# Converting the feed-forward weights later and more thinly inside a top-k attention and gated feed-forward kernel

## The chip, the cores and the metric

The kernel runs on one core of a Trainium2 chip. The metric is the time of one execution on the device, in microseconds (us). The engines of the core are TensorE (PE, with its weight loads as PEld), VectorE (DVE), ScalarE (ACT), GpSimd (POOL) and SyncE (SP, which here issues all DMAs).

## The reference

Attention over 8 batches of 8 heads, 576 positions, head size 64. Each row keeps its 32 largest scores; the result is the input of a feed-forward block with a convolution over three positions as its gate. The inputs q, k, v are float32, the weights float64.

```python
scores = scale * np.matmul(q, k.transpose(0, 1, 3, 2))
kth = np.partition(scores, -top_k, axis=-1)[..., -top_k:-top_k + 1]
scores = np.where(scores >= kth, scores, -1000000000.0)
attn = softmax(scores)                        # written out in the reference
x = np.matmul(attn, v)                        # (8, 576, 512) after the heads are joined
h = np.maximum(x @ w_in, 0.0)                 # w_in 512 x 1024
conv_out = sum(conv_w[k] * shifted(h, k - 1) for k in range(3))
out = (h * 1.0 / (1.0 + np.exp(-conv_out))) @ w_out      # w_out 1024 x 512
```

## The kernel before

The work is cut into 288 attention tiles of 128 rows by 576 scores: 8 batches, 4 pairs of heads, 9 tiles a pair. A software pipeline runs over them. Iteration `it` (from -3 on) issues one stage of each of several tiles, in an order written out by hand in `iteration`; each engine runs its own instructions in just that order. For tile n the stages are: the scores on PE and their copy to memory by ACT (L218, L225) two iterations ahead; seven MAX8 over chunks on DVE at it = n (L232); five further DVE steps that narrow the candidates at n + 1 (L252, L254); the sign of each score against a threshold by ACT (`sides`, L265) and its product on POOL (`flip`, L270) at n + 2; the exponential by ACT (`expo`, L277) at n + 3; a last MAX8, the choice of the threshold and the masked weights on DVE at n + 4 (`below` L280, `select` L284, `weigh` L290); the transposes on PE (L303) and their copy at n + 5 (L308); then the product with v (L334). So the start of L290 for tile i marks iteration i + 4, and L290 is executed once in each iteration from 4 to 291.

After the nine tiles of a pair the sums are inverted on DVE (L349, L350) and sent through DRAM by SP (L358 to L364). POOL then normalises in three operations (L369 to L371) that wait in a list, `pool_tasks`. A budget decides how many of that list an iteration runs: 2.0 an iteration, less `CONV_COST` 1.5 for each weight block on POOL. When the fourth pair of a batch is normalised, the feed-forward work of the batch starts: `Expand` (L401, one of eight blocks of 128 features every two iterations, for each of two parts of the rows), the gate (L470 on DVE), `Contract` (L551). The gated activations lie in memory under the tags g0 and g1, one for each part.

The float64 weights arrive as pairs of 32-bit words. 33 blocks (conv_w, then 16 of w_in, then 16 of w_out, 128 x 256 values each) are loaded by SP (L141) and converted, one block an iteration from iteration -3. A block passes through `split` on DVE (L149, a shift of the upper word), `act` on ACT (L152, L153), `pool` on POOL one iteration later (L157 the sign, L158 an integer add, L159 the product), `lead` on ACT in that same iteration (L162, the rounded high part), and `trail` on POOL an iteration later (L165, the low part). The raw words use the buffers of the tags x_hi and x_lo, which later hold the normalised rows; the temporaries lie in `scratch`, three slots of four. `load_blocks` keeps up to 12 blocks loaded ahead. `Expand` waits until the blocks of w_in are done, and `split_next`, ahead of `Contract`, until all are.

Of the kernel before, what the change touches and what calls it, by code (L numbers as in the profile page):

```python
# [13 lines left out]
BF16 = mybir.dt.bfloat16  # L14
U16 = mybir.dt.uint16
U32 = mybir.dt.uint32
I32 = mybir.dt.int32
AF = mybir.ActivationFunctionType
ALU = mybir.AluOpType
ENG = mybir.EngineType  # L20

P = 128
# [10 lines left out]
XNB = 7  # L33
# [12 lines left out]
FEED = 1.42  # L46
CONV_COST = 1.5
W_FIRST = 4
W_LATE = 12
NORM_LAG = 2  # L50
CONV_LAG = 1
OB = 1
WB = 256
# [12 lines left out]
def attend_and_feed(ctx: ExitStack, tc: tile.TileContext, q, k, v, weights, out, shared, finish=None):  # L66
    nc = tc.nc
# [5 lines left out]
    DM, DF = wi.shape[2] * P, wi.shape[3]  # L73
    NCT = DM // P
    NFT = DF // P
# [7 lines left out]
    ROWS = [(0, NI * TAIL), (NI * TAIL, S)]  # L83
# [6 lines left out]
    xp = ctx.enter_context(tc.tile_pool(name="xp", bufs=XNB))  # L90
    moe = ctx.enter_context(tc.tile_pool(name="moe", bufs=1))
# [10 lines left out]
    for i in range(0 if exact else SB):  # L102
        side = const.tile([P, S + 3], BF16, name=f"side{i}")
# [15 lines left out]
    def bank(name):  # L119
        return ps.tile([P, BANK], F32, name=name, tag=name, bufs=1)  # L120
# [1 line left out]
    def corner(i):  # L122
        return s_ps[:, i * (P + S):i * (P + S) + P]

    scratch = []

    class Convert:
        count = 0
# [4 lines left out]
        def load(self):  # L133
            i = Convert.count
            Convert.count += 1
            if not scratch:
                scratch.append(moe.tile([P, 4 * SPB, WB], F32, name="scratch", tag="split"))
            self.at = i % SPB * 4
            tag = ("x_hi", "x_lo")[i % 2]
            self.raw = xp.tile([P, self.src.shape[-1], 2], U32, name="raw64", tag=tag)[0:self.n]  # L140
            nc.sync.dma_start(out=self.raw.rearrange("a c t -> a (c t)"), in_=self.src.bitcast(U32))  # L141

        def tmp(self, i):
            return scratch[0][0:self.n, self.at + i, 0:self.raw.shape[1]]

        def split(self):
            self.bits, self.rest, self.side = (self.tmp(i) for i in range(3))
            top = self.raw[:, :, 1]
            yield lambda: nc.vector.tensor_scalar(self.bits.bitcast(U32), top, 3, None, ALU.logical_shift_left)  # L149

        def act(self):
            nc.scalar.activation(out=self.rest, in_=self.raw[:, :, 0], func=AF.Copy, scale=2.0 ** -51, bias=2.0)  # L152
            nc.scalar.activation(out=self.side.bitcast(I32), in_=f32(self.raw[:, :, 1]), func=AF.Copy, scale=0.5 / LEAST)  # L153

        def pool(self):
            x, side = self.bits, self.side
            nc.gpsimd.tensor_scalar(side, side.bitcast(I32), 1.0, -1.0, ALU.min, ALU.max)  # L157
            nc.gpsimd.tensor_tensor(x.bitcast(U32), x.bitcast(U32), self.rest.bitcast(U32), ALU.add)  # L158
            nc.gpsimd.tensor_tensor(self.dst if self.low is None else x, x, side, ALU.mult)  # L159

        def lead(self):
            nc.scalar.copy(out=self.dst, in_=self.bits)  # L162
# [4 lines left out]
    def weight_blocks():  # L167
        w_in, conv_w, w_out = weights
        yield Convert(conv_w, P, cw.rearrange("p t f -> p (t f)"), None)
        for c in range(NCT):  # L170
            for n in range(0, DF, WB):
                yield Convert(w_in[c * P:(c + 1) * P, n:n + WB], P, wi[:, 0, c, n:n + WB], wi[:, 1, c, n:n + WB])
        for f in range(NFT):
            for n in range(0, DM, WB):
                yield Convert(w_out[f * P:(f + 1) * P, n:n + WB], P, wo[:, 0, f, n:n + WB], wo[:, 1, f, n:n + WB])
# [4 lines left out]
    def ratios():  # L180
        size(cr[:, 0], cw[:, 1])
        nc.vector.tensor_scalar(cr[:, 0], cr[:, 0], SMALL, None, ALU.is_lt)
        nc.vector.tensor_tensor(cr[:, 0], cr[:, 0], cw[:, 1], ALU.add)
        nc.vector.reciprocal(cr[:, 0], cr[:, 0])
        nc.vector.tensor_tensor(cr[:, 1], cr[:, 0], cw[:, 2], ALU.mult)
        nc.vector.tensor_tensor(cr[:, 0], cr[:, 0], cw[:, 0], ALU.mult)
# [306 lines left out]
    class Contract:  # L493
# [11 lines left out]
        def split(self):  # L505
# [3 lines left out]
            if late and len(parts) == 1:  # L509
                for pool, name, n, size in ((att, "e2", EBUFS, 2 * S), (att, "pT", 2, 2 * MAIN)):  # L510
                    for _ in range(n):
                        t = pool.tile([P, size], F32R, name=name, bufs=n)
                        extra.append(t[:, 0:2 * NFT * TAIL].rearrange("p (i c) -> p i c", i=2))
                parts.extend(extra)
# [95 lines left out]
        return expands.popleft()  # L610

    def next_contract():
        if not contracts or not contracts[0].ready:
            return None
        if contracts[0].first:
            if contracted.waiting >= (2 if state.it > NT + 4 else CB):
                return None
            contracted.waiting += 1
        return contracts.popleft()
# [13 lines left out]
    expands, contracts = deque(), deque()  # L633
    state = Box()
    state.flying = state.avs = state.it = 0
    state.due, state.tanh_at = 0.0, -9
    state.split = state.splits = state.late_splits = 0
    state.credit, state.pool = 0.0, 0.0
    lanes = expanded, contracted = Box(), Box()
    for lane, take in zip(lanes, (next_expand, next_contract)):  # L640
        lane.take, lane.cur, lane.waiting, lane.finished = take, None, 0, deque()
# [2 lines left out]
    blocks = deque()  # L644
    if weights is not None:
        blocks.extend(weight_blocks())
    state.blocks = 0 if weights is not None else NCT * DF
    fetched, cut, dved, whole, led = (deque() for _ in range(5))

    def start(pc):  # L650
# [22 lines left out]
                    lane.finished.append(lane.unit)  # L673
        return budget

    def load_blocks(n=2 * XNB - 3):
        while blocks and len(fetched) < n:
            c = blocks.popleft()
            c.load()
            fetched.append(c)  # L680

    def convert_pool():
        while led:
            led.popleft().trail()
            state.blocks += 1
        while dved:
            c = dved.popleft()
            c.pool()
            if c.low is None:
                state.blocks += 1  # L690
                ratios()
            else:
                whole.append(c)

    def convert_dve():
        ops = []
        if fetched:
            c = fetched.popleft()
            ops.extend(c.split())
            cut.append(c)  # L700
        return ops

    def convert_act():
        while cut:
            c = cut.popleft()
            c.act()
            dved.append(c)
        while whole:
            c = whole.popleft()
            c.lead()  # L710
            led.append(c)
        load_blocks(W_LATE)

    av_next, out_next, rec_next, norm_wait = [], [], [], []

    def iteration(it):
        nonlocal av_next, out_next, rec_next
        n = it + 3
# [14 lines left out]
        if n < NT:  # L733
# [3 lines left out]
            t = Box()  # L737
# [18 lines left out]
        else:  # L756
            a_ops = list(chunk_ops(tA)) if tA is not None else []
            b_ops = list(cand_ops(tB)) if tB is not None else []
        pool_used = CONV_COST * len(dved)
        convert_pool()  # L760
        c_ops = convert_dve()
        for i in range(max(7, len(a_ops), len(b_ops))):
            if i < len(a_ops):
                a_ops[i]()
# [58 lines left out]
        while pool_tasks and state.pool > 0.2 and pool_tasks[0][0] <= it:  # L823
# [3 lines left out]
            _, c, fn = pool_tasks.popleft()  # L827
# [6 lines left out]
    with tc.manual_schedule(engines=engines) if engines else nullcontext():  # L834
        load_blocks(1)
        fetch(pcs[0])
        load_blocks(W_FIRST)
        fetch(pcs[1])
        for it in range(-3, NT + 6):
            iteration(it)  # L840
    if finish is not None:
        finish(corner(2)[0:1, 0:1])
    while expands or contracts or any(x.waiting for x in lanes) or pool_tasks or tanh_next or tanh_now or gates:
        it += 1
        iteration(it)
# [3 lines left out]
def kernel(  # L849
# [32 lines left out]
    def count_lost(total):  # L882
# [19 lines left out]
        nc.vector.tensor_copy(flag, total)  # L902

    attend_and_feed(tc, q, k, (v_main, v_tail), (w_in, conv_w, w_out), out, shared, count_lost)
    lost_rows = nc.values_load(flag[0:1, 0:1])
    with tc.If(lost_rows > 0):
        attend_and_feed(tc, q, k, (v_main, v_tail), None, out, shared)
# [55 lines left out]
```

## Time and profile before

| | |
|---|---|
| median of 3 runs | 1115.03 us (1114.95 to 1115.05) |
| profiled execution, own time | 1114.6 us |
| its span on the core | 1112.7 us |
| busy share of the span | PE 90%, PEld 73%, DVE 92%, ACT 89%, POOL 80% |

The span runs from the first to the last instruction of the profiled execution; its own time is 1.9 us longer. Engines overlap, so the shares don't add up; and the share of the whole span is a mean over stages that need not have the same limit.

### The profile page before, as it was taken

How to read it: one execution, taken by the hardware profiler on the slowest of the kernel's cores; microseconds unless marked ns; L12 is line 12 of the kernel's file. 1: busy time of each engine (PE TensorE's matmuls, PEld its weight loads, DVE VectorE, ACT ScalarE, POOL GpSimd, SP SyncE). 2: the span in 40 equal slices, each digit the busy share in tenths (PEclk: the TensorE clock that was granted, in tenths of full speed). 3: DMA queues.
4: the chain of work that ended last, by engine and by line, in shares of the span. 5: the costliest groups of instructions: out<-in, count | busy, mean ns of one | idle time of the engine just before them, and what ended most of it. 6: DMA issues, size and time to landing. Idle time of an engine off the chain costs nothing.

```text
span 1112.7 us, 28088 instructions
## 1 busy us (share of the span) xinstructions
PE 1006.6 (90%) x8354; PEld 810.4 (73%) x8354; DVE 1024.9 (92%) x5768; ACT 989.6 (89%) x2342; POOL 892.1 (80%) x1078
## 2 busy tenths in 40 slices
PE   3666568889999999999999899999999999999997
PEld 2444456667788787888788777888778777887985
DVE  5998999999999999999999999999999999998551
ACT  5998888999999999999999999999999999998442
POOL 6999956889888897999887997978988897999200
PEclk9986899999999999999999999999999999999998
DMA  7221011111111111111111111111111111000001
GB/s 256 90 90 45 2 44 46 46 45 45 64 46 55 55 32 40 49 55 56 55 55 61 50 53 32 40 51 55 55 55 55 55 55 47 29 24 22 31 29 41
DMA packets 51697, 58.70 MB, mean 53 GB/s; under 512 B 9776, under 2 KB 30544, under 8 KB 51536
## 3 DMA queue, kind: packets, MB, share of 16 engines
q1 hardware_dynamic: 51536, 56.82, 16.0%
q8 instruction: 69, 1.13, 0.4%
q14 instruction: 92, 0.75, 0.2%
HBM read 47.21 MB, written 9.58 MB: 51 GB/s over the span
## 4 chain that ended last, share of the span: by engine, by line
PE 45%; DVE 38%; ACT 12%; POOL 3%; issue 2%; DMA 0%; SPq 0%; ACTq 0%; POOLq 0%
DVE cand L232 12%; PE mc L551 10%; PE me L401 9%; DVE e L290 9%; DVE z L280 7%; PE pt L303 6%; PE s_ps L334 6%; PE s_ps L218 6%; DVE cand L254 3%; ACT weights_ps L277 3%; ACT side L265 2%; PE weights_ps L551 2%; DVE rows L252 2%; DVE hot L284 2%; ACT rows L225 2%; PE s_ps L207 2%
## 5 line engine op out<-in xcount | busy, mean ns | idle before, releaser
L232 DVE MAX8 cand<-rows 128x8 f32<-128x82 f32 (+1 forms) x2016 | 453.2, 239 | 1.1 <-ACT rows L225 1.1
L270 POOL TENSOR_TENSOR z<-rows,side 128x579 f32<-128x579 f32 x288 | 347.8, 1207 | 110.4 <-ACT side L265 88.7
L277 ACT ACTIVATE weights_ps<-rows,z 128x576 f32<-128x576 f32 x288 | 219.6, 762 | 16.1 <-DVE e L290 7.5
L290 DVE SCALAR_TENSOR_TENSOR e<-rows,kth,weights_ps 128x576 f32<-128x576 f32 x288 | 230.4, 800 | 0.2
L265 ACT ACTIVATE side<-rows 128x576 bf16<-128x576 f32 x288 | 224.5, 779 | 0.3
L401 PE MATMUL me<-x_hi,wi 128*128 128x322 f32 (+1 forms) x928 | 218.3, 308 | 2.4 <-ACT g L415 1.6
L280 DVE MAX8 z<-z 128x8 f32<-128x576 f32 x288 | 214.2, 744 | 1.5 <-POOL z L270 1.5
L218 PE MATMUL s_ps<-k,q 64*128 64x384 f32 (+1 forms) x1024 | 172.5, 450 | 43.8 <-ACT xt L345 28.1
L225 ACT COPY rows<-s_ps 128x576 f32<-128x576 f32 x288 | 183.2, 636 | 21.0 <-PE s_ps L337 13.7
L303 PE MATMUL pt<-ident,e 128*128 128x128 f32 x1152 | 195.1, 293 | 2.6 <-DVE e L290 2.3
L334 PE MATMUL s_ps<-pT,vn 128*64 128x128 f32 (+1 forms) x2560 | 167.1, 274 | 26.1 <-ACT rows L225 26.0
L551 PE MATMUL mc<-wo,split 128*128 128x512 f32 x684 | 187.1, 407 | 0.2 <-ACT o L567 0.2
L218 PEld LDWEIGHTS s_ps<-k,q 64*128 64x128 f32 x1024 | 122.1, 191 | 86.2 <-ACT xt L345 37.0
L334 PEld LDWEIGHTS s_ps<-pT,vn 128*64 128x64 f32 x2560 | 130.7, 140 | 62.2 <-ACT rows L225 33.4
L303 PEld LDWEIGHTS pt<-ident,e 128*128 128x128 f32 x1152 | 125.1, 145 | 57.2 <-issue 28.9
L401 PEld LDWEIGHTS me<-x_hi,wi 128*128 128x128 f32 x928 | 156.7, 189 | 4.7 <-ACT g L415 2.8
L308 ACT COPY pT<-pt 128x512 f32<-128x512 f32 x256 | 154.6, 604 | 0.7 <-PE pt L303 0.7
L401 PE MATMUL me<-x_lo,wi 128*128 128x258 f32 (+1 forms) x464 | 138.3, 298 | 0.0
L551 PEld LDWEIGHTS mc<-wo,split 128*128 128x128 f32 x684 | 120.1, 189 | 20.4 <-ACT o L567 0.6
L434 POOL TENSOR_SCALAR t<-g,cr 128x256 f32<-128x256 f32 (+1 forms) x222 | 114.4, 515 | 0.0
L252 DVE MAX8 rows<-cand 128x8 f32<-128x21 f32 x576 | 109.6, 190 | 0.0
L448 POOL TENSOR_TENSOR t<-t,t 128x256 f32<-128x256 f32 (+1 forms) x111 | 89.2, 803 | 9.2
(116 smaller groups left out, 1673.6 us busy)
## 6 DMA issues: line engine op xcount, KB each, us to landing
k<-in_k_dram SPq DMA_DIRECT2D x32, 288.0 KB
q<-in_q_dram SPq DMA_DIRECT2D x32, 288.0 KB
vn<-in_v_main_dram SPq DMA_DIRECT2D x32, 256.0 KB
rb<-row SPq DMA_DIRECT2D x64, 128.0 KB
out_dram<-o SPq DMA_DIRECT2D x24, 256.0 KB
raw<-in_w_in_dram SPq DMA_DIRECT2D x16, 256.0 KB
raw<-in_w_out_dram SPq DMA_DIRECT2D x16, 256.0 KB
vt<-in_v_tail_dram SPq DMA_DIRECT2D x32, 64.0 KB
```

The source lines that it names most:

```text
L218: made.append(nc.tensor.matmul(s_ps[:, to + a:to + z], lhsT=qx[rows_of[h], at], rhs=kx[rows_of[h], a:z], start=True, stop=True))
L225: nc.scalar.copy(out=x, in_=s_ps[:, at:at + S])
L232: yield lambda c=c, at=at, n=n: nc.vector.max(out=t.cand[:, c:8 * CHUNKS:CHUNKS], in_=t.x[:, at:at + n])
L265: nc.scalar.activation(out=t.side[:, 2:S + 2], in_=t.x, func=AF.Sign, scale=-OVER, bias=t.row[:, 7:8], accum_out=t.cnt)
L270: nc.gpsimd.tensor_tensor(t.z[:, 8:S + 11], t.row[:, 6:S + 9], t.side, ALU.mult)
L277: nc.scalar.activation(out=e_ps, in_=t.x, func=AF.Exp, scale=scale, bias=t.shift)
L280: nc.vector.max(out=t.z[:, 0:8], in_=t.z[:, 10:S + 10])
L290: nc.vector.scalar_tensor_tensor(out=t.e, in0=t.x, scalar=kth[:, t.n:t.n + 1], in1=e_ps, op0=ALU.is_ge, op1=ALU.mult, accum_out=t.pc.sums[ ...
L303: nc.tensor.transpose(tp[:, i * P:(i + 1) * P], t.e[:, o + i * P:o + (i + 1) * P], ident)
L334: nc.tensor.matmul(a[r, 0:w], lhsT=st.pc.vn[:, h, i], rhs=st.pT[:, h if st.i < NI else 1 - h, i, 0:w], start=(i == 0), stop=False)
L401: nc.tensor.matmul(mm[:, 0:w], lhsT=wt, rhs=xx, start=(n == 0), stop=(n == len(ops) - 1))
L551: nc.tensor.matmul(mm[0:m], lhsT=x[:, i], rhs=wo[:, e, f], start=start, stop=stop)
```

## The change

The raw words go into five slots of one tile under the tag g1, which the feed-forward work writes only later, and four blocks at most are loaded ahead (12 before). conv_w is converted at iteration -3 as before. Then a counter, `state.turn`, holds the others back until iteration 2 and lets three of every four iterations convert a block. The shift becomes a SCALAR_TENSOR_TENSOR whose second operand is a block of zeros in PSUM (the bank "mc", set once by a MEMSET). The sign is written as bf16 into the fourth temporary of the slot, and the order on POOL is sign and add of the new block, `trail` of the block before, then the product. `next_contract` waits for all blocks too.

```diff
-W_LATE = 12
+W_LATE = 4
+RAWS = 5
+RATE = 0.75
...
+        nil = bank("mc").bitcast(U32)
+        nc.vector.memset(nil[:, 0:WB], 0)
...
-            tag = ("x_hi", "x_lo")[i % 2]
-            self.raw = xp.tile([P, self.src.shape[-1], 2], U32, name="raw64", tag=tag)[0:self.n]
+            if not raws:
+                raws.append(moe.tile([P, NFT * (ROWS[1][1] - ROWS[1][0] + 4)], U32, name="raw64", tag="g1"))
+            to = i % RAWS * 2 * WB
+            self.raw = raws[0][0:self.n, to:to + 2 * self.src.shape[-1]].rearrange("p (c t) -> p c t", t=2)
...
-            self.bits, self.rest, self.side = (self.tmp(i) for i in range(3))
+            self.bits, self.rest, self.side, sign = (self.tmp(i) for i in range(4))
+            self.sign = sign.bitcast(BF16)[:, 0:sign.shape[1]]
             top = self.raw[:, :, 1]
-            yield lambda: nc.vector.tensor_scalar(self.bits.bitcast(U32), top, 3, None, ALU.logical_shift_left)
+            yield lambda: nc.vector.scalar_tensor_tensor(out=self.bits.bitcast(U32), in0=top, scalar=3,
+                                                         in1=nil[0:self.n, 0:top.shape[1]],
+                                                         op0=ALU.logical_shift_left, op1=ALU.bitwise_or)
...
-        def pool(self):
-            x, side = self.bits, self.side
-            nc.gpsimd.tensor_scalar(side, side.bitcast(I32), 1.0, -1.0, ALU.min, ALU.max)
-            nc.gpsimd.tensor_tensor(x.bitcast(U32), x.bitcast(U32), self.rest.bitcast(U32), ALU.add)
-            nc.gpsimd.tensor_tensor(self.dst if self.low is None else x, x, side, ALU.mult)
+        def add(self):
+            x = self.bits.bitcast(U32)
+            nc.gpsimd.tensor_scalar(self.sign, self.side.bitcast(I32), 1.0, -1.0, ALU.min, ALU.max)
+            nc.gpsimd.tensor_tensor(x, x, self.rest.bitcast(U32), ALU.add)
+
+        def signed(self):
+            nc.gpsimd.tensor_tensor(self.dst if self.low is None else self.bits, self.bits, self.sign, ALU.mult)
...
-        if not contracts or not contracts[0].ready:
+        if not contracts or not contracts[0].ready or state.blocks < 1 + 2 * NCT * DF // WB:
...
-    def load_blocks(n=2 * XNB - 3):
+    def load_blocks(n):
...
     def convert_pool():
+        for c in dved:
+            c.add()
         while led:
             led.popleft().trail()
             state.blocks += 1
         while dved:
             c = dved.popleft()
-            c.pool()
+            c.signed()
...
-        c_ops = convert_dve()
+        state.turn += RATE
+        c_ops = []
+        if state.turn >= 1.0 or not fetched:
+            c_ops = convert_dve()
+            state.turn -= 1.0 if it > -3 else 1.0 + RATE * 4
```

## Rows read from the trace of the kernel before

**Rows 1.** Windows: start:end, length, busy of PE, PEld, DVE, ACT, POOL, clock, DMA.

```profile
0.00:25.74 25.74, 9.17 (x32) 6.97 (x32) 13.83 (x100) 13.98 (x34) 16.51 (x37) 1.00 0.82 276
25.74:135.30 109.56, 69.19 (x516) 50.68 (x516) 102.64 (x546) 98.68 (x248) 106.29 (x142) 0.86 0.18 58
135.30:180.31 45.01, 32.01 (x298) 23.45 (x298) 44.82 (x269) 40.08 (x96) 24.22 (x22) 0.92 0.18 56
```

**Rows 2.** Timeline of DVE, L290 alone: start, duration (tiles 0, 27, 41).

```profile
25.74 0.80 DVE L290 SCALAR_TENSOR_TENSOR e<-rows,kth,weights_ps 128x576 f32<-128x576 f32 x1
...
135.30 0.80 DVE L290 SCALAR_TENSOR_TENSOR e<-rows,kth,weights_ps 128x576 f32<-128x576 f32 x1
...
180.31 0.80 DVE L290 SCALAR_TENSOR_TENSOR e<-rows,kth,weights_ps 128x576 f32<-128x576 f32 x1
```

**Rows 3.** Timeline of POOL: start, duration; one iteration with a block.

```profile
59.77 0.40 POOL L157 TENSOR_SCALAR scratch<-scratch 128x256 f32<-128x256 int32 x1
60.14 0.72 POOL L158 TENSOR_TENSOR scratch<-scratch 128x256 uint32<-128x256 uint32 x1
60.94 0.74 POOL L159 TENSOR_TENSOR scratch<-scratch 128x256 f32<-128x256 f32 x1
61.63 1.21 POOL L270 TENSOR_TENSOR z<-rows,side 128x579 f32<-128x579 f32 x1
62.79 0.78 POOL L165 TENSOR_TENSOR wi<-scratch,wi 128x256 fp32r<-128x256 f32 x1
```

**Rows 4.** Groups of POOL, 25.74 to 180.31: flip and the normalisation.

```profile
L270 POOL TENSOR_TENSOR z<-rows,side 128x579 f32<-128x579 f32 x42 | 50.8, 1211 | 20.6 <-ACT side L265 10.2 <-DVE cand L232 4.6 <-issue 3.8
...
L369 POOL TENSOR_TENSOR xt<-xt,rb 128x576 f32<-128x576 f32 x4 | 5.6, 1410 | 0.0
L370 POOL TENSOR_SCALAR x_hi<-xt 128x576 fp32r<-128x576 f32 x4 | 2.8, 692 | 0.0
```

**Rows 5.** Timeline of DVE and POOL: an early shift; a flip and the shift beside it.

```profile
8.89 0.28 DVE L149 TENSOR_SCALAR scratch<-raw 128x256 uint32<-128x256 uint32 x1
...
42.80 1.20 POOL L270 TENSOR_TENSOR z<-rows,side 128x579 f32<-128x579 f32 x1
...
43.48 0.67 DVE L149 TENSOR_SCALAR scratch<-raw 128x256 uint32<-128x256 uint32 x1
```

**Rows 6.** Groups of DVE, 25.74 to 180.31: the shift.

```profile
L149 DVE TENSOR_SCALAR scratch<-raw 128x256 uint32<-128x256 uint32 x25 | 17.1, 682 | 0.0
```

**Rows 7.** Timeline of DVE: a gate (SBUF and PSUM operands) and the weighing behind it.

```profile
226.51 0.41 DVE L470 SCALAR_TENSOR_TENSOR g<-weights_ps,g 128x256 f32<-128x256 f32 x1
226.83 0.81 DVE L290 SCALAR_TENSOR_TENSOR e<-rows,kth,weights_ps 128x576 f32<-128x576 f32 x1
```

**Rows 8.** Timeline of ACT at the start of the kernel.

```profile
7.48 0.64 ACT L225 COPY rows<-s_ps 128x576 f32<-128x576 f32 x1 [4.54 <-PE s_ps L218]
8.01 0.43 ACT L152 ACTIVATE scratch<-raw 128x256 f32<-128x256 uint32 x1
...
8.67 0.63 ACT L225 COPY rows<-s_ps 128x576 f32<-128x576 f32 x1
```

**Rows 9.** Timeline of PE and POOL: the second group of scores, and the first flip.

```profile
9.35 2.29 PE L218 MATMUL s_ps<-k,q 64*128 64x192 f32 x8 [1.91 <-ACT rows L225]
...
20.30 1.20 POOL L270 TENSOR_TENSOR z<-rows,side 128x579 f32<-128x579 f32 x1
```

**Rows 10.** Groups of ACT, 25.74 to 180.31: sign and exponential.

```profile
L265 ACT ACTIVATE side<-rows 128x576 bf16<-128x576 f32 x42 | 32.5, 773 | 0.1
L277 ACT ACTIVATE weights_ps<-rows,z 128x576 f32<-128x576 f32 x41 | 30.7, 749 | 3.3 <-DVE e L290 2.0 <-DVE rec L350 0.8 <-POOL z L270 0.4
```

**Rows 11.** Instructions of L551: min/median/max ns, first and last start.

```profile
L551 PE MATMUL mc<-wo,split x684: 388/394/499, 257.2 to 1037.7; 128*128 128x512 f32 x171
```

**Rows 12.** Timeline of SP: the sums' way through DRAM, and a load behind it.

```profile
62.97 0.35 SPq L358 DMA_DIRECT2D row<-rT  x1
...
69.79 0.36 SPq L141 DMA_DIRECT2D raw<-in_w_out_dram  x1
```

More of the change, by code (lines that the diff above doesn't have):

```diff
@@ L123, in corner @@
         return s_ps[:, i * (P + S):i * (P + S) + P]
-    scratch = []
+    scratch, raws = [], []
+    if weights is not None:
+        nil = bank("mc").bitcast(U32)
+        nc.vector.memset(nil[:, 0:WB], 0)
     class Convert:
@@ L637, in attend_and_feed @@
     state.split = state.splits = state.late_splits = 0
-    state.credit, state.pool = 0.0, 0.0
+    state.credit, state.pool, state.turn = 0.0, 0.0, 1.0
     lanes = expanded, contracted = Box(), Box()
@@ L646, in attend_and_feed @@
         blocks.extend(weight_blocks())
-    state.blocks = 0 if weights is not None else NCT * DF
+    state.blocks = 0 if weights is not None else 2 * NCT * DF
     fetched, cut, dved, whole, led = (deque() for _ in range(5))
```

## The prediction

> **What bounds the kernel now.** The table of busy shares comes first: DVE leads with 92%, but POOL's 80% is a mean over stages, so the windows by stage come next. From tile 0's weighing (iteration 4) to tile 27's (iteration 31) POOL is busy 106.3 of 109.6 us [rows 1]; the next 14 iterations, without blocks, keep DVE busy 44.8 of 45.0 us and POOL only 24.2 [rows 1]. The weighings give the pace: 25.74, 135.30 and 180.31 us for tiles 0, 27 and 41 [rows 2], so 109.56 / 27 = 4.06 us an iteration with a block and 45.01 / 14 = 3.215 without (the few inversions of sums included). The timeline of POOL shows why: one iteration with a block runs sign, add, product, flip, `trail` end to end from 59.77 to 62.79 + 0.78 = 63.57, 3.8 us [rows 3]. Two normalisations fall in the stretch, each about 1.41 + 0.69 + 1.41 = 3.5 us (L371 counted like L369, a subtraction of the same size) [rows 4]; 27 x 3.78 + 7.0 = 109.1 against the 109.56 measured. So POOL alone sets the pace up to iteration 31, DVE from there to iteration 45, and the change can gain only by iteration 45 or so. What the feed-forward work then sets is left alone.
>
> **The change part by part.** I sum from the start of the profile to the weighing of tile 41 (iteration 45), 180.31 us before.
>
> Blocks after the change: the counter gives conv_w at iteration -3, then iterations 2, 3, 4, 6, 7, 8 and so on, 32 blocks, the last at 43. Behind the weighing of tile 0 lie 29 shifts, and POOL's part of 31 blocks.
>
> *Start.* Before, blocks run on POOL and ACT from iteration -2, and the first flip waits until 20.30 [rows 9]. Without them the chain is ACT and PE in turn. A copy of scores holds ACT about 0.53 (7.48 to 8.01), the two steps of `act` 0.66 (8.01 to 8.67) [rows 8]. Tile 1's copy moves from 8.67 to 8.01 and ends at 8.64; the next scores take 2.29 [rows 9], to 10.95; two copies to 12.0; scores to 14.3; then on ACT tile 4's copy 14.85, `act` 15.5, a sign 0.77 [rows 10] to 16.3, tile 5's copy 16.8, `act` 17.5, `lead` (of `act`'s size, 0.33) 17.8, the exponential 0.75 [rows 10] to 18.6, and `select` with `weigh` behind it: estimate 19.3 for tile 0. DVE and POOL are earlier than that. Gain 25.74 - 19.3 = 6.4 us; I allow 1.5 us either way.
>
> *DVE to tile 41.* The 41 iterations cost 41 x 3.215 = 131.8 us. The new shift, one SBUF and one PSUM operand, has its nearest row in the gate, 256 wide with such operands: 0.41 us, and 0.32 from its start to the next instruction's [rows 7]. Bounds: 0.28, the old shift at its best, and 0.80, the weighing of 576 columns [rows 5, 7]. With 0.32: 29 x 0.32 = 9.3, sum 141.1 us.
>
> The old shift takes 0.28 at 8.89, and 0.68 in the mean of 25 [rows 5, 6]. The one beside the flip starts at 43.48 and ends at 44.15, just behind the flip's end at 44.00 [rows 5]: it waited for POOL. The Trainium skill, "SBUF — State Buffer", section "SBUF: two separate sides", says that an exclusive lock on a port pair is held for a whole instruction, by POOL or by a DVE instruction in a two-port mode or with two SBUF inputs; the new form is neither. By that rule the wait disappears. That same skill, "VectorE: DVE Perf Modes", section "Why PSUM operands drop a tier", speaks against the edit: any PSUM operand holds fp32 at one element a cycle. An estimate by it is 256 / 0.96 GHz = 0.27 us of streaming instead of 0.13, 0.13 x 29 = 4 us more on DVE than the old shift alone; no run here shows the new form yet.
>
> *POOL to tile 41.* 42 flips at 1.16 from start to start (61.63 to 62.79) [rows 3] are 48.7. A block: sign 0.37, add 0.80 before (60.14 to 60.94) for an instruction of 0.72, since the product behind it needs its result; now `trail` stands between, so 0.69, as from the product to the flip; `trail` 0.76, product 0.69 [rows 3]: 2.51. Reading the sign as bf16 may shorten the product: a flip with one bf16 operand takes 1.21 where two f32 operands take 1.41 [rows 4], in proportion 0.1 us of a block. I take half. Writing bf16 is not shown; bounds: nothing, and 0.29, the gap between L370's 0.69 and L157's 0.40 [rows 3, 4]; I take nothing, as L157 has the same input and size. 31 x 2.46 + 48.7 + 4 x 3.5 = 139.0 us, 2 us under DVE.
>
> *ACT to tile 41.* 40.08 / 14 = 2.86 busy us an iteration without blocks [rows 1], 41 x 2.86 = 117.3; a block adds 0.66 + 0.33 = 0.99, 29 x 0.99 = 28.7: 146.0 us. That is an upper reading, for neighbouring instructions overlap a little where they are back to back.
>
> So after the change DVE 141, POOL 139 and ACT at most 146 lie together, each in a fixed order and waiting for the others. I take the middle of 141.1 and 146.0, 143.6 us. Tile 41: 19.3 + 143.6 = 162.9, against 180.31: a gain of 17.4 us. The profiled execution (1114.6, a span of 1112.7 with 1.9 around it) becomes 1097.2; the median of the runs lies 0.4 higher: 1097.6 us.
>
> *Edits at nothing.* The MEMSET of the zeros lies on DVE before the first scores have been copied at 7.48, an idle time [rows 8]; uncovered, it costs a few tenths once. Contraction first touches bank "mc" at 257.2 [rows 11], 90 us after the last shift, and with it the later end of the conversion and the new gate in `next_contract` are covered: they would cost only past that margin. g1 is written after part 0's eight expansions, 16 iterations behind the batch's start, so its loan as raw buffer is over. Loads now stand one by one on SP's queue behind k, q, v and the sums' way through DRAM; a wait there lasted 62.97 to 69.79, 6.8 us, until a load behind it was issued [rows 12]; four blocks ahead are over five iterations, some 18 us, which covers that. Nothing else on SP waits for a load that isn't ready to go: its slot was read by `act` an iteration before. The last normalisation of batch 0 shares POOL's budget with a block (2.0 - 1.5 leaves 0.5), so the feed-forward work starts one iteration later; its 16 expansions at every second iteration leave four iterations of 36 free, and I count nothing. With that slack gone it would be one iteration, 3.2 us.
>
> **The rivals.**
> - *No loss to coupling.* The buffers between engines absorb everything, and DVE's 141.1 holds with a start 1 us earlier: tile 41 at 159.4, 1094 us. For: without blocks DVE loses almost nothing [rows 1]. Against: three engines close to full.
> - *POOL stays the bound.* The bf16 write costs 0.29 and the order hides nothing (0.11 a block): 139.0 + 31 x (0.29 + 0.05 + 0.11) = 153, tile 41 at about 172, gain 8: 1107 us. For: POOL's writes of fp32r are slow [rows 4]. Against: L157 converts its type already.
> - *The shift still waits for POOL.* By the old shift's 0.68 + 0.13, less its overlap, some 0.7 instead of 0.32: 29 x 0.38 = 11, 1109 us. For: the mean of 25 old shifts shows the wait [rows 6]; against: the gate, with the new form's kinds of operands, takes its 0.41 [rows 7].
> - *Slower: the shift as a three-operand integer instruction on words eight bytes apart is dear.* Place: DVE, in the conversion's 29 iterations. The gain is gone at 0.32 + 17.4 / 29 = 0.92 us a shift; at 1.33, four times the gate's hold, the kernel ends near 1127 us. No row shows integers in this form; the 576-wide weighing needs 0.80 only.
> - *The change does nothing measurable:* the later blocks meet the feed-forward's first iterations and lose what was gained; this needs about 17 us from batch 0 alone, and POOL's blocks have ended by then.
>
> **How the numbers follow.** Chances: forecast (1096 to 1102) 0.53; no loss 0.15; POOL bound 0.12; shift waits 0.10; same 0.04; slower 0.06. The predicted time is the forecast's, 1097.6. The range goes from 1093 (no loss, the start at its early bound) to 1108, which leaves out half of the shift's rival, same and slower, and a little of the lowest: 2 in 10. A measurement here tells about 0.2% (2.2 us) from no change. Faster 0.53 + 0.15 + 0.12 + 0.10 = 0.90, same 0.04, slower 0.06.
>
> **What would show it.** Right: tile 0 weighed near 19.3, tile 41 near 163; the shift at 0.4 and steady wherever POOL is; plain iterations of 3.2 and others of about 3.5; POOL with gaps before the flip. From tile 50 on the spacing is that of before. Wrong: POOL without gaps and its sign above 0.6 (bound), a shift whose end follows a POOL instruction's end (lock), the start held by a transfer, or a first contraction that comes later, beside the rest, than the tiles do.

## The result and the profile after

The changed kernel takes 1101.51 us (1099.52 to 1102.43) against 1114.99 before, a ratio of 0.988 with a 95% interval of 0.987 to 0.989: 13.5 us less, where 17.4 were forecast and 1097.6 us predicted. Beside the second group of experiments it took 1099.72, a ratio of 0.9865 (0.985 to 0.988). The execution profiled below took 1102.43 us of its own, 12.2 less than the 1114.6 profiled before.

Windows of the changed kernel, cut at the weighings of tiles 0, 27 and 41; the columns are those of [rows 1]:

```profile
0.00:19.85 19.85, 9.16 (x32) 6.98 (x32) 12.35 (x96) 9.83 (x22) 6.20 (x22) 1.00 0.55 180
19.85:116.08 96.23, 59.59 (x518) 43.79 (x516) 93.88 (x541) 91.59 (x231) 88.40 (x117) 0.95 0.27 88
116.08:164.65 48.57, 32.97 (x298) 24.63 (x298) 48.00 (x278) 47.69 (x124) 44.90 (x59) 0.89 0.26 80
```

Timeline of DVE in the changed kernel, the weighings of tiles 0, 27, 41, 47 and 50 (L302 is the former L290), beside [rows 2]:

```profile
19.85 0.80 DVE L302 SCALAR_TENSOR_TENSOR e<-rows,kth,weights_ps 128x576 f32<-128x576 f32 x1
...
116.08 0.80 DVE L302 SCALAR_TENSOR_TENSOR e<-rows,kth,weights_ps 128x576 f32<-128x576 f32 x1
...
164.65 0.80 DVE L302 SCALAR_TENSOR_TENSOR e<-rows,kth,weights_ps 128x576 f32<-128x576 f32 x1
...
184.12 0.80 DVE L302 SCALAR_TENSOR_TENSOR e<-rows,kth,weights_ps 128x576 f32<-128x576 f32 x1
...
195.27 0.79 DVE L302 SCALAR_TENSOR_TENSOR e<-rows,kth,weights_ps 128x576 f32<-128x576 f32 x1
```

The gain grows along the tiles: 5.9 us at tile 0, 19.2 at tile 27, where the kernel before ended its conversion; then 3.6 are given back, since the conversion goes on while the kernel before was free of it, which leaves 15.7 at tile 41. POOL, which left 3.3 of 109.56 us idle in [rows 1], now leaves 7.8 of 96.23; DVE leaves 2.3. So DVE now has the least idle time, though over the 41 iterations to tile 41 (144.8 us) DVE with 141.9 us busy, ACT with 139.3 and POOL with 133.3 lie close together.

Groups of the changed kernel, 19.85 to 164.65, first of POOL and then of DVE; they answer to [rows 3, 6]:

```profile
L282 POOL TENSOR_TENSOR z<-rows,side 128x579 f32<-128x579 f32 x41 | 49.5, 1207 | 3.1 <-ACT side L277 2.9
L168 POOL TENSOR_TENSOR scratch<-scratch 128x256 uint32<-128x256 uint32 x31 | 22.6, 728 | 0.0
L171 POOL TENSOR_TENSOR scratch<-scratch 128x256 f32<-128x256 f32 x31 | 20.9, 673 | 0.8
L167 POOL TENSOR_SCALAR scratch<-scratch 128x256 bf16<-128x256 int32 x30 | 12.1, 402 | 7.5 <-ACT scratch L163 7.5
```

```profile
L157 DVE SCALAR_TENSOR_TENSOR scratch<-raw,mc 128x256 uint32<-128x256 uint32 x29 | 11.6, 401 | 0.0
```

These rows show the shift at 0.401 us where it was 0.682, and POOL waiting for ACT 7.5 us in front of the sign: POOL has time to spare. The new order shows in POOL's timeline of the changed kernel:

```profile
59.75 0.72 POOL L168 TENSOR_TENSOR scratch<-scratch 128x256 uint32<-128x256 uint32 x1
60.43 0.73 POOL L177 TENSOR_TENSOR wi<-scratch,wi 128x256 fp32r<-128x256 f32 x1
61.12 0.68 POOL L171 TENSOR_TENSOR scratch<-scratch 128x256 f32<-128x256 f32 x1
61.74 1.22 POOL L282 TENSOR_TENSOR z<-rows,side 128x579 f32<-128x579 f32 x1
```

From add to the next instruction it is 0.68 us, where add and product stood 0.80 apart in [rows 3]; the product is 0.68 instead of 0.74.

### The profile page after: what moved, and what is told of

Read it like the earlier page. It is cut to its first block, busy times and chain, and to the rows that moved or that the text cites. A ratio compares the mean times of both kernels' runs of the same rounds, so it can differ in the third digit from the quotient of the medians.

```text
span 1100.5 us, 28065 instructions
## 1 busy us (share of the span) xinstructions
PE 1002.3 (91%) x8354; PEld 809.4 (74%) x8354; DVE 1019.3 (93%) x5769; ACT 986.7 (90%) x2342; POOL 887.3 (81%) x1078
## 4 chain that ended last, share of the span: by engine, by line
PE 48%; DVE 35%; ACT 12%; POOL 2%; issue 2%; DMA 0%; SPq 0%; ACTq 0%; POOLq 0%
DVE cand L244 11%; PE me L413 10%; PE mc L563 9%; DVE e L302 8%; PE s_ps L346 7%; PE pt L315 7%; PE s_ps L230 6%; DVE z L292 6%; DVE cand L266 3%; ACT weights_ps L289 2%; ACT side L277 2%; PE weights_ps L563 2%; ACT rows L237 2%; DVE rows L264 2%; DVE hot L296 2%
## 5 line engine op out<-in xcount | busy, mean ns | idle before, releaser
L302 DVE SCALAR_TENSOR_TENSOR e<-rows,kth,weights_ps 128x576 f32<-128x576 f32 x288 | 229.9, 798 | 0.2
L413 PE MATMUL me<-x_hi,wi 128*128 128x322 f32 (+1 forms) x928 | 223.0, 312 | 2.3 <-ACT g L427 1.6
```

The source lines that it names most:

```text
L302: nc.vector.scalar_tensor_tensor(out=t.e, in0=t.x, scalar=kth[:, t.n:t.n + 1], in1=e_ps, op0=ALU.is_ge, op1=ALU.mult, accum_out=t.pc.sums[ ...
L413: nc.tensor.matmul(mm[:, 0:w], lhsT=wt, rhs=xx, start=(n == 0), stop=(n == len(ops) - 1))
```

## The experiments

All but the repetition differ from the changed kernel (or, the third, from the kernel before) by the edit shown. Tile times are the weighings in the one profile of each. The kernels ran in groups, and each ratio is to the kernel before as it ran in the same group (medians 1113.89 to 1114.99 us), so across groups the ratios are to be compared and not the medians. With the hold at the start in place, tile 0 lies between 19.29 and 20.03 without any edit that bears on it; the two profiles of the changed kernel differ by 0.48 us there and by 0.15 at tile 41.

| kernel | median us | ratio to before (95%) | tile 0 | tile 41 | tile 47 to 50 | tile 287 |
|---|---|---|---|---|---|---|
| before | 1114.99 | | 25.74 | 180.31 | 10.17 | 1022.02 |
| changed | 1101.51 | 0.9879 (0.9866 to 0.9892) | 19.85 | 164.65 | 11.15 | 1008.73 |
| changed, again | 1099.72 | 0.9865 (0.985 to 0.988) | 19.37 | 164.50 | 11.04 | 1008.10 |
| old shift | 1103.06 | 0.9895 (0.988 to 0.9911) | 19.29 | 166.18 | 9.85 | 1008.74 |
| zeros in SBUF | 1105.51 | 0.9922 (0.9909 to 0.9936) | 19.36 | 169.24 | 9.84 | 1011.15 |
| before with new shift | 1113.18 | 0.9986 (0.9977 to 0.9995) | 25.29 | 178.04 | 10.16 | 1020.36 |
| schedule only | 1108.18 | 0.9936 (0.9923 to 0.995) | 19.79 | 171.39 | 11.14 | 1015.31 |
| old POOL part | 1104.41 | 0.9912 (0.9899 to 0.9926) | 19.43 | 168.24 | 9.85 | 1010.46 |
| f32 sign | 1102.99 | 0.99 (0.9883 to 0.9916) | 19.47 | 165.62 | 11.19 | 1009.13 |
| old POOL order | 1102.72 | 0.9896 (0.988 to 0.9913) | 19.29 | 166.52 | 9.85 | 1008.70 |
| every iteration | 1107.09 | 0.9934 (0.9921 to 0.9948) | 20.03 | 169.25 | 10.17 | 1012.02 |
| no hold | 1101.66 | 0.9891 (0.9874 to 0.9908) | 21.27 | 164.84 | 10.17 | 1007.72 |
| more PE work | 1101.33 | 0.9887 (0.9872 to 0.9902) | 19.73 | 165.25 | 9.84 | 1006.99 |
| more PE work, later | 1099.41 | 0.9866 (0.985 to 0.9883) | 19.37 | 163.71 | 9.84 | 1006.51 |

**The old shift put back.**

```diff
-            yield lambda: nc.vector.scalar_tensor_tensor(out=self.bits.bitcast(U32), in0=top, scalar=3,
-                                                         in1=nil[0:self.n, 0:top.shape[1]],
-                                                         op0=ALU.logical_shift_left, op1=ALU.bitwise_or)
+            yield lambda: nc.vector.tensor_scalar(self.bits.bitcast(U32), top, 3, None, ALU.logical_shift_left)
```

> The changed kernel with the old one-operand shift put back, all else kept. Theory (the shift of the old form waits for POOL's running instruction and so holds DVE, which sets the pace after the change): the shift's mean goes from 0.40 to about 0.7 us, 29 x 0.3 = 9 us more to tile 41, some 1109 to 1111 us. Rival (the form of the shift is of no matter once POOL has gaps; the old form is even shorter when nothing is in its way): 1099 to 1102 us.

1103.06 us, between the two forecasts; tile 41 comes 1.5 to 1.7 us later, not 9. Its shifts, in the groups of DVE:

```profile
L157 DVE TENSOR_SCALAR scratch<-raw 128x256 uint32<-128x256 uint32 x29 | 15.9, 549 | 0.0
```

They take 0.549 us in the mean, 0.15 more than the new form, 29 x 0.15 = 4.3 us of DVE in all, of which other waits hide more than half. The theory holds in kind: some shifts wait; a stretch of its timeline, DVE and POOL, shows one beside the first operation of a normalisation, which ends at 68.05:

```profile
60.41 0.36 DVE L157 TENSOR_SCALAR scratch<-raw 128x256 uint32<-128x256 uint32 x1
...
66.65 1.40 POOL L379 TENSOR_TENSOR xt<-xt,rb 128x576 f32<-128x576 f32 x1
...
67.19 1.01 DVE L157 TENSOR_SCALAR scratch<-raw 128x256 uint32<-128x256 uint32 x1
```

But in the new schedule other shifts meet less of POOL, and the old form is then the shorter one. In time the two kernels can't be told apart for sure: the intervals overlap, and at tile 287 they stand level.

**The zeros in SBUF.**

```diff
-        nil = bank("mc").bitcast(U32)
-        nc.vector.memset(nil[:, 0:WB], 0)
+        nil = const.tile([P, WB], U32, name="nil")
+        nc.vector.memset(nil, 0)
```

> The changed kernel with the zeros in SBUF instead of PSUM, the same instruction otherwise. If a second operand read from SBUF is what makes DVE and POOL exclude each other: shift mean 0.6 to 0.8 us, tile 41 later by 6 to 11 us, 1107 to 1112 us. If only the faster one-operand mode did so: shift 0.40, 1100 to 1103 us.

1105.51 us, tile 41 4.6 to 4.7 later: less than the 6 to 11 expected, though the shift's mean lies in its range. DVE's shifts take 7.6 us more over the stage; 1.7 of that are taken out of DVE's idle time, which falls from 2.9 to 1.2 us. The same instruction with both operands in SBUF waits; groups of DVE, and then a stretch of the timeline, DVE and POOL:

```profile
L157 DVE SCALAR_TENSOR_TENSOR scratch<-raw,nil 128x256 uint32<-128x256 uint32 x29 | 19.2, 662 | 0.0
```

```profile
40.07 1.20 POOL L282 TENSOR_TENSOR z<-rows,side 128x579 f32<-128x579 f32 x1 [0.24 <-ACT side L277]
...
40.18 1.38 DVE L157 SCALAR_TENSOR_TENSOR scratch<-raw,nil 128x256 uint32<-128x256 uint32 x1
...
58.71 0.97 POOL L171 TENSOR_TENSOR scratch<-scratch 128x256 f32<-128x256 f32 x1
...
58.74 0.42 DVE L157 SCALAR_TENSOR_TENSOR scratch<-raw,nil 128x256 uint32<-128x256 uint32 x1
```

At 40.18 the shift starts 0.11 behind the flip and ends at 41.56, 0.29 behind the flip's end at 41.27. At 58.74 it goes at its 0.42, and POOL's product beside it takes 0.97 instead of 0.67, although its record begins 0.03 earlier. So it is either the one or the other that waits, and in this form of instruction it is the second SBUF operand that does it: with that operand in PSUM the shift stays at 0.40. The Trainium skill, "SBUF — State Buffer", section "SBUF: two separate sides", names a DVE instruction with two SBUF inputs among those that exclude a POOL instruction that reads SBUF; this trace agrees, 0.662 us against 0.401.

**The new shift alone, in the kernel before.**

```diff
+    if weights is not None:
+        nil = bank("mc").bitcast(U32)
+        nc.vector.memset(nil[:, 0:WB], 0)
...
-            yield lambda: nc.vector.tensor_scalar(self.bits.bitcast(U32), top, 3, None, ALU.logical_shift_left)
+            yield lambda: nc.vector.scalar_tensor_tensor(out=self.bits.bitcast(U32), in0=top, scalar=3,
+                                                         in1=nil[0:self.n, 0:top.shape[1]],
+                                                         op0=ALU.logical_shift_left, op1=ALU.bitwise_or)
```

> The kernel before with the new shift alone. Theory (POOL sets the pace before, 3.78 us an iteration with a block): at most the POOL instruction that stood beside a shift gets shorter, 0.05 x 27, so 1112 to 1115 us, and DVE has idle time in front of select. Rival (the shift's waits were the loss): 27 x 0.3 = 8 us and more, 1104 to 1107 us.

1113.18 us, 0.14% less: as the theory has it. Windows of this kernel from tile 0 to tile 27:

```profile
25.29:133.12 107.83, 66.93 (x516) 49.04 (x516) 97.20 (x546) 98.57 (x248) 104.91 (x142) 0.84 0.19 59
```

DVE's busy time falls by 5.4 us against [rows 1], the stretch by 1.7 only: POOL still has 104.9 of 107.8 us filled, and what DVE saves turns into waiting.

**The schedule and the place of the raw words only.** The edit is that of the old shift above, that of the f32 sign and that of the old POOL order below, together.

> The changed kernel with the old shift, the old order on POOL and the f32 sign: only the later and thinner schedule and the place of the raw words are left of the change. Theory (each part takes a term of its own): tile 0 at 20 as in the changed kernel, iterations with a block at 3.8 on DVE and POOL, tile 41 at about 19.9 + 29 x 3.8 + 12 x 3.2 + 3 = 171.5, so 1108 to 1111 us. Rival (the schedule alone makes the gain): 1100 to 1103 us.

1108.18 us, tile 41 at 171.39: half of the gain is the schedule's, half that of the three edits on POOL and DVE. How much the place of the raw words and the smaller number of blocks loaded ahead do by themselves was not run. This kernel differs from the one with the old POOL part (below) by the shift alone, and there the new shift is worth 3.2 us at tile 41 (171.39 against 168.24), twice the 1.5 to 1.7 beside the new POOL part: the edits overlap, and their single prices don't add up.

**The changed kernel again.** No edit.

> The changed kernel once more, beside the three others on one chip. If the 1.3 us that its profile lost between tiles 47 and 50, at a granted clock of 0.58, are an accident of that execution, tile 287 comes 1.3 us earlier than 1008.73; if they belong to the kernel, they come again. Time 1099 to 1102 us.

1099.72 us; tile 47 to 50 takes 11.04 us again, so the loss there is no accident of one execution.

**The old POOL part, and its two halves.** The first of these kernels has both edits, the other two one each.

```diff
-            self.sign = sign.bitcast(BF16)[:, 0:sign.shape[1]]
+            self.sign = sign
```

```diff
-        for c in dved:
-            c.add()
         while led:
             led.popleft().trail()
             state.blocks += 1
         while dved:
             c = dved.popleft()
+            c.add()
             c.signed()
```

> The changed kernel with the old order on POOL and the f32 sign; schedule and new shift are kept. Theory (with the shift off POOL's ports, POOL's block at 2.5 instead of 2.35 us still fits under DVE): tile 41 at 165 to 168, 1102 to 1105 us. Rival (POOL's share of the change is worth as much here as it was beside the old shift, where tile 41 moved by 5.2 us): 1106 to 1108 us.

> The changed kernel with the sign in f32, the new order on POOL kept. Theory (the product alone gets longer, 0.67 to 0.73 us, 2 us over the stage, most of it in POOL's gaps): tile 41 0.5 to 1.5 us later than 164.6, 1100 to 1102 us. Rival (the bf16 sign is what made POOL's part): tile 41 at 168, 1103 to 1105 us.

> The changed kernel with the old order on POOL, the bf16 sign kept. Theory (the gap between add and product, 0.1 us, and the wait of lead for a later product are the larger part): tile 41 2 to 3.5 us later than 164.6, 1102 to 1104 us. Rival (order is of no matter): 1099 to 1101 us.

Both back: 1104.41 us, tile 41 3.6 to 3.7 later. The sign alone moves tile 41 by 1.0 to 1.1, the order alone by 1.9 to 2.0; their intervals of time overlap with each other. So the order is the larger half there, as expected, though a little under its 2 to 3.5; the sign's 1102.99 us lies above its 1100 to 1102, and with both back tile 41 lies just past its 165 to 168. At tile 287 the old order stands level with the changed kernel (1008.70 against 1008.73 and 1008.10), mostly because the changed kernel loses 1.2 to 1.3 us against it between tiles 47 and 50 (see *More work on PE*). In the groups of POOL of the kernel with both back, 19.5 to 166 us:

```profile
L171 POOL TENSOR_TENSOR scratch<-scratch 128x256 f32<-128x256 f32 x31 | 22.5, 727 | 2.4
L168 POOL TENSOR_TENSOR scratch<-scratch 128x256 uint32<-128x256 uint32 x31 | 22.5, 727 | 0.0
L167 POOL TENSOR_SCALAR scratch<-scratch 128x256 f32<-128x256 int32 x31 | 12.4, 399 | 3.9 <-ACT scratch L163 3.9
L177 POOL TENSOR_TENSOR wi<-scratch,wi 128x256 fp32r<-128x256 f32 x16 | 11.6, 727 | 3.2 <-ACT wi L174 3.2
```

The pause in front of the product is 2.4 us over the stage against 0.8, and `trail`, first in POOL's queue, waits 3.2 us for `lead` on ACT, which it never does in the new order, where it stands behind sign and add. Not all of that wait is saved: in the new order POOL waits for ACT 7.5 us in front of the sign, in the old one 3.9.

**A block in every iteration.**

```diff
-RATE = 0.75
+RATE = 1.0
```

> The changed kernel with a block in every iteration from 2 on instead of three of four. Theory (POOL's 3.5 us in an iteration with a block leave no room for the normalisations, which then lengthen the pace): 19.9 + 30 x 3.54 + 2 x 3.5 + 12 x 3.2, tile 41 at about 171.5, 1107 to 1109 us. Rival (only DVE's sum counts, which is the same): 1100 to 1103 us.

1107.09 us. From tile 0 to tile 27:

```profile
20.03:122.22 102.19, 60.18 (x516) 44.20 (x516) 97.30 (x547) 97.62 (x250) 102.19 (x142) 0.93 0.30 93
```

POOL is busy without a pause and sets the pace again: 27 x 3.54 us and two normalisations of 3.5 make 102.6, against 102.19. At tile 41, 13 iterations behind the last block on DVE (the counter begins at iteration 1 with this rate), 4.6 to 4.8 us remain lost, where the forecast of 171.5 had 7. DVE's sum is the same as with three in four, so it is not that sum alone that counts, but also whether POOL has room for the normalisations.

**No hold at the start.**

```diff
-            state.turn -= 1.0 if it > -3 else 1.0 + RATE * 4
+            state.turn -= 1.0
```

> The changed kernel without the hold: three blocks in four iterations from iteration -2 on. Theory (blocks before the first weighing lie on the chain of ACT, PE and POOL; tile 0 at 22 to 23, about 1 us given back by three shifts fewer behind it): tile 41 at 166 to 167, 1101.5 to 1103.5 us. Rival (the hold only moves work; its sum is the same): tile 41 at 164.6, 1099 to 1101 us.

1101.66 us, tile 41 at 164.84. The time would fit the theory, but the tiles do not: tile 0 comes at 21.27 instead of 22 to 23, and at tile 41 the rival holds. Tile 0 comes 1.4 to 1.9 us later, and by tile 41 0.2 to 0.3 of that is left, since three shifts fewer lie behind tile 0 and the conversion ends sooner.

**More work on PE.** Four transposes of the identity in each iteration, into the half of bank mc that isn't used.

```diff
-        nil = bank("mc").bitcast(U32)
+        mc = bank("mc")
+        nil = mc.bitcast(U32)
+        warm_ps = mc[:, 2 * WB - P:2 * WB]
...
+        if weights is not None and 4 <= it <= 47:
+            for i in range(4):
+                nc.tensor.transpose(warm_ps[:, 0:P], ident, ident)
```

> The changed kernel with four more transposes of the identity a iteration on PE, into the unused half of bank mc, in iterations 4 to 47; their result is not used. Theory (the iterations above 3.5 at tiles 18 to 27 and 47 to 50 come from stretches at the granted clock of 0.5): clock 1.00 from 20 to 190 us, these iterations near 3.5, 2 to 4 us less, 1097 to 1100 us. Rival (they come from waits between ACT, POOL and DVE, or from more work on PE): no gain or a loss, 1101 to 1105 us.

The second kernel begins at iteration 12:

```diff
-        if weights is not None and 4 <= it <= 47:
+        if weights is not None and 12 <= it <= 47:
```

> The kernel with extra transposes on PE once more, from iteration 12 to 47 alone. Theory (with them from iteration 4 the third interval was 4.87 us, which is their price there; later they keep the clock at 1.00 and cost nothing): tile 41 at 164, tile 50 at 193.5, 1097.5 to 1099.5 us. Rival (what the clock gives back is lost to PE's longer queue): 1100 to 1102 us.

Windows around the start of the feed-forward work, first of the changed kernel and then of the one with PE work from iteration 12:

```profile
176.00:180.00 4.00, 2.12 (x28) 1.61 (x26) 4.00 (x23) 3.85 (x12) 2.51 (x4) 1.00 0.02 4
180.00:184.00 4.00, 4.00 (x24) 3.48 (x21) 4.00 (x29) 2.86 (x7) 3.55 (x6) 0.58 0.19 54
```

```profile
176.00:180.00 4.00, 2.79 (x33) 2.18 (x32) 4.00 (x29) 3.84 (x11) 3.20 (x5) 1.00 0.01 1
180.00:184.00 4.00, 3.84 (x48) 2.96 (x46) 4.00 (x23) 3.47 (x10) 3.85 (x6) 1.00 0.29 79
```

In the changed kernel PE has been busy 2.1 of 4 us, the granted clock falls, and over the expansion it is 0.58 in the mean, a mixture of the levels of 1.2 and 2.4 GHz; with the added work it stays at 1.00. Tile 47 to 50 then takes 9.84 us instead of 11.04 to 11.15.

But the added work is not needed for that. Of the eight kernels whose feed-forward work starts between tiles 42 and 43 without it, the four with a clock of 0.73 to 0.74 between tiles 45 and 47 (the changed kernel, its repetition, schedule only, f32 sign) take 11.04 to 11.19 us from tile 47 to 50, and the four at 1.00 (old shift, zeros in SBUF, old POOL part, old POOL order) take 9.84 or 9.85. Windows from tile 44 to 45 and from 45 to 47, first of the changed kernel and then of the one with the old shift:

```profile
174.21:177.78 3.57, 2.53 (x18) 1.81 (x17) 3.50 (x22) 2.93 (x9) 2.08 (x4) 1.00 0.02 5
177.78:184.12 6.34, 5.50 (x42) 4.69 (x44) 6.34 (x39) 5.04 (x14) 5.68 (x8) 0.73 0.13 37
```

```profile
175.74:179.32 3.58, 2.54 (x19) 1.82 (x17) 3.51 (x22) 2.94 (x9) 2.09 (x4) 1.00 0.02 5
179.32:185.66 6.34, 5.50 (x71) 4.49 (x72) 6.34 (x40) 5.78 (x15) 6.02 (x9) 1.00 0.12 35
```

PE is as busy before the fall in the one as in the other, so its work there does not tell by itself whether the clock falls; what decides it stays open. What the fall costs is plain from these eight: about 1.3 us.

For the rest the theory fails. The slow iterations of 3.9 at tiles 18, 25 and 27 stay with a clock of 1.00; those at 18 and 27 are a plain 3.5 and an inversion of sums, 0.4. And with the added work from iteration 4 on, the clock is not at 1.00 from 20 us on: it falls at 24 us, and the interval from tile 1 to 2 takes 4.88 us instead of 3.53. A window of that kernel there (in the changed kernel that interval has a clock of 1.00):

```profile
24.00:28.00 4.00, 3.98 (x23) 2.90 (x23) 2.73 (x20) 2.92 (x7) 3.89 (x5) 0.57 0.19 48
```

So the 1.4 us lost there can be the price of the added work, as the second expectation has it, or of the clock; no run separates the two. From iteration 12 on, time and tile times come as that expectation says (1099.41 us; tile 41 at 163.71, tile 50 at 192.97). Still, 1099.41 and 1101.33 us do not differ clearly from the changed kernel, 1099.72 and 1101.51.

## Why the prediction was right, and where it was too high

- *POOL bounds before, DVE after*: right. The new shift alone gains 0.14%; a block in every iteration makes POOL the bound again; the windows after show DVE 2.3 us short of full up to tile 27. That DVE alone sets the pace is too much said: of what the old shift and the zeros in SBUF add to DVE, 4.3 and 7.6 us, tile 41 moves by 1.5 to 1.7 and 4.6 to 4.7.
- *The start*: 19.3 forecast, 19.85 and 19.37 measured: the cause was right. But the hold is no gain of its own: without it tile 41 comes level. The term was right at tile 0 and is paid back within the sum that followed it.
- *DVE to tile 41*: 141.1 us forecast, 141.9 busy measured. The shift was priced at 0.41 and measured 0.40, 0.12 more than the old one at its best, near the 0.13 estimated against the edit; iterations of 3.50 with a block and 3.17 without are what 0.32 on top of 3.2 says.
- *POOL to tile 41*: 139.0 forecast, 133.3 busy measured. The write of bf16 costs nothing, 402 ns beside 399; the product loses 0.05 us, as taken; the order's gap of 0.1 closes. The bound of 0.29 for that write was no price: it compared L370, 576 columns wide, with L157, 256 wide, and neither row shows a write of fp32r to be slow. What the sum left out is `trail` waiting for `lead`, 5.3 us of idle time with the old part (3.2 for w_in, 2.1 for w_out) and none after. That this is why the old POOL part costs 3.6 us at tile 41, though its sum would fit under DVE, is likely and not shown: the old order alone has the same waits, 5.4 us, and costs 1.9 to 2.0.
- *Coupling*: 143.6 taken, 144.8 and 145.1 measured. This came near partly by luck. The 143.6 are the middle between DVE's 141.1 and ACT's 146.0, but ACT was busy for 139.3 us only, less than DVE: its term was 6.7 us too large. What was measured is DVE's 141.9 and 2.9 us in which it waited.
- *The rival that the shift still waits*: its price, 11 us, was too high by far. The new form with its zeros in SBUF does wait, by 0.26 us a shift in the mean where the rival had 0.38, and costs 4.6 to 4.7 us at tile 41. The old form, put back, costs 1.5 to 1.7; its mean of 0.68 in the kernel before, where POOL had hardly a pause, is 0.55 here.
- *What was counted at nothing*: here is the missing part. "Starts one iteration later" was right (the first expansion starts at 169.9, between tiles 42 and 43; before at 182.0, between 41 and 42), and the iteration as such costs nothing; but in both profiles of the changed kernel PE's clock falls just then, and tile 47 to 50 loses 1.0 us against before. The four kernels with the same start of that work and a clock of 1.00 lose nothing there. From tile 50 to 287 another 0.8 to 1.4 go. Of that, 0.3 is where the cut falls, since the expansions come at every second iteration and start one iteration later; and the kernel before with the new shift, whose work is that of before by then, takes 0.6 more than the kernel before itself, so about as much is a difference between executions. The rest stays open. And the stretch from the issue of the last outputs to the end of the span is longer, 1092.16 to 1100.5 against 1105.45 to 1112.7, 1.1 us, at work that the change does not touch; it varies from kernel to kernel, and by 0.7 between the two profiles of the changed kernel, and stays open.

So 17.4 forecast become 15.7 at tile 41 by the start and the coupling, 14.6 at tile 50 with the fall of the clock, 13.3 at tile 287, 12.2 in this profile's span. In the medians the gain is 13.5.

## What to carry to other kernels

Preparatory work that shares engines with a pipeline should be thinned until its engine has room for the bursts that come anyway (here the normalisations), not merely until the mean fits: three blocks in four iterations gained 4.6 us at tile 41 and 7.4 in the medians against one in each, with the same sum. On an engine that runs in order, try an independent instruction between two that depend on each other, and a later place for one that waits for another engine: here that order gained 1.9 to 2.0 us at tile 41. A fix for a wait is worth what the critical path loses by it, and that depends on the rest: the shift's 0.28 us of waiting was plain in the trace, and removing it was worth 1.7 us in the kernel before, 3.2 at tile 41 with the new schedule and the old POOL part, and 1.5 to 1.7 beside the new one.

## What the runs showed of the hardware

A SCALAR_TENSOR_TENSOR of 256 columns on DVE with one operand in SBUF and one in PSUM took 0.40 us and never above 0.43, whatever POOL did; with both in SBUF it took 0.66 in the mean and up to 1.38, and POOL's product beside it once 0.97 instead of 0.67. POOL multiplies 256 f32 columns in 0.73 us, and in 0.67 if one operand is bf16. A granted clock of 0.73 to 0.74 over two iterations, just as new work starts on PE, costs about 1.3 us here; the same PE work before it was followed by a fall in four kernels and by none in four others.
